# Joining seven expert accumulators later: stored raw, then added by GpSimd in the last network

## Chip, cores and metric

The kernel runs on one core of one Trainium2 chip. The metric is the device time of one execution in microseconds (us). TensorE does the matrix products, VectorE and ScalarE the elementwise work, GpSimd elementwise work on SBUF only, and SP's queue issues most transfers.

## The reference

The program chains three networks over 2304 tokens: an attention with random features, a mixture of eight experts, and a last two-layer network. Only the last two touch the change:

```python
# experts: x is (2304, 512), w1 (8, 512, 1024), w2 (8, 1024, 512)
out = np.zeros((N, D), dtype=np.float32)
for e in range(E):
    h = np.maximum(x @ w1[e], 0.0)
    ye = h @ w2[e]
    out += P[:, e:e + 1] * ye        # P: gate weights, after 8 rounds of normalisation
# last network: w_in (512, 2048), w_out (2048, 512)
h = x @ w_in
g = h - np.tanh(h)
return (g @ w_out).astype(np.float32)
```

All data are float32. The kernel splits each operand into a high part and a low part and takes three products (high x high, high x low, low x high) for each one above.

## The kernel before

Tokens are worked in three blocks of 768 (two halves of 384). The stages run in this order: attention; the experts for blocks 0, 1, 2; the last network for blocks 0, 1, 2.

**The experts in blocks 1 and 2.** The 8 x 1024 hidden units are cut into 32 quads of 256. A quad is multiplied by a scheme of seven products in place of eight (Strassen, in Winograd's form). `quad7` does the first layer: seven products into three PSUM banks, with gates and ReLU on VectorE, and seven operands `h7_*`, each split into high (ScalarE, L1286) and low (GpSimd, L1289). The second layer multiplies each of the seven operands by its own weights and sums over the quads into seven accumulators `seven0` to `seven6` in SBUF (`xacc`, 128 x 2 x 384 each, 384 KB). `group` is one such product for one half `d` of the rows. Where its flag `act` is set and the accumulator holds something, ScalarE first copies the accumulator into the PSUM bank (`pre`, L1372), the products add to it there, and ScalarE copies the bank back (L1396). Otherwise VectorE adds bank and accumulator (L1400). `second_layer` puts a quad's groups into a plan of numbered slots; `slot(t)` issues what is due at t, seven slots to a quad, and the second layer of a quad runs in the slots of the next.

**The end of a block.** The seven sums have to be combined into four results. In the last quad (`r == NQ - 1`) the groups get a list `outs`: each bank is preloaded with its own accumulator, and evicted by VectorE into another (L1394), for instance `xacc[3] <- bank` by ScalarE beside `xacc[5] <- bank + xacc[5]` by VectorE. `join` then has GpSimd make two more additions (L1416) and stores four results (L1413) into the DRAM tensor `xd[1]`, three on SP and one on ScalarE's queue. After block 1 this stands between the last quad of one block and the first of the next. After block 2 it stands in front of the last network: the eleven slots left over are spread over the first four `p` products of block 0 there, three, four and four at a time, through `second(...)`.

**The last network.** Groups of four hidden slices (`GF = 4`) and two token halves give half-groups. A half-group has four `shrink` calls (twelve `p` products each, L1481, an activation built from ScalarE and VectorE operations, L1493 to L1504, and a split of the hidden value into high on ScalarE, L1509, and low on GpSimd, L1510) and, some time later, three `l2` calls (twelve `l` products each, L1521, evicted by VectorE, L1546 or L1548). In `weights` the jobs `"i"` split the first layer's weights on GpSimd (`u`, L110), four units to a load, and the jobs `"s"` the second layer's (`v`), half on GpSimd and half on VectorE. `tick` advances these generators, `wprep` and `xprep`, one step.

**The next block's x.** `xops` (the generator `xprep`) loads the x of the coming block and splits it into units, by turns on VectorE and GpSimd (L110). For the last network it waits until `(1, s)` is in `xdone` and `xgo` allows it, that is, until the first group of the block before has been issued.

The lines that matter most:

```python
def pre():
    cell.append(lbank(f"Y{t}_{i}_{d}")[:, :TB])
    nc.scalar.copy(cell[0], xacc[i][:, d])
...
        one(4, 3, [(5, 5), (3, None)])
...
        at(t + 7)[2].extend((put(4, 0, 0), add(3, 2)))
        at(t + 8)[2].append(add(5, 1))
```

Of the kernel before, what the change touches and what calls it, by code (L numbers as in the profile page):

```python
# [20 lines left out]
def performer_moe_kernel(ctx, tc, q, k, v, omega, wg, w1, w2, win64, wout64, out):  # L21
# [6 lines left out]
    P = 128  # L28
# [47 lines left out]
    pt = con.tile([P, NTT, E], F32, name="pt")  # L76


    stages = [(0, s) for s in range(NSB)] + [(1, s) for s in range(NSB)]
# [95 lines left out]
    def second_units(R):  # L175
        r = R % NQ
        if r == 0:
            return [(0, R), (2, R), (1, R), (6, R), (3, R)]
        if r % 2 == 0:
            return [(0, R - 1), (0, R), (3, R), (2, R), (1, R), (6, R - 1), (6, R)]  # L180
        units = [(5, R - 1), (5, R), (4, R - 1), (4, R), (3, R), (2, R), (1, R)]
        return [(0, R), *units, (6, R)] if r == NQ - 1 else units

    def weights():
# [10 lines left out]
        for s in range(NSB):  # L195
            for g in range(NGM):
                for f in range(g * GF, (g + 1) * GF, 2):
                    jobs.append(("i", 0, lambda f=f: load_win(f), NCV if s else made["i", f]))
                for f in range(g * GF, (g + 1) * GF):
                    jobs.append(  # L200
                        (
                            "s",
                            -1,
                            lambda f=f: load_slab(wout32[f * P : (f + 1) * P, :]),
                            NCV if s else made["o", f],
                        )
                    )
# [38 lines left out]
        while ahead or jobs:  # L246
# [75 lines left out]
            elif k == "i":  # L322
                raw, done = raw
                for i in range(4):
                    while not free1(n1):
                        yield 1
                    o = i // 2 * P
                    unit1(n1, raw[:, i % 2 * 2 : i % 2 * 2 + 2, o : o + P], nc.gpsimd)
                    n1 += 1
                    yield None  # L330
# [31 lines left out]
    def xops():  # L362
        nx = 0
        order = []
        for k, (kind, s) in enumerate(stages):
            src = xd[kind].rearrange("(i c p) t -> p i c t", p=P, i=2)
            t0 = s * SBT
            opening = k == 0
            while not (opening or ready_x(kind, s) and k <= xgo[0]):
                yield 1  # L370
            b = {}

# [993 lines left out]

    def group(t, i, gs, d, act, first, last, outs=()):
        cell = []
# [5 lines left out]
        def run():  # L1374
# [13 lines left out]
            def evict():  # L1388
                if outs:
                    for x, y in outs:  # L1390
                        if y is None:
                            nc.scalar.copy(xacc[x][:, d], ps)
                        else:
                            nc.vector.tensor_tensor(xacc[x][:, d], ps, xacc[y][:, d], ALU.add)  # L1394
                elif act:
                    nc.scalar.copy(xacc[i][:, d], ps)  # L1396
# [6 lines left out]

        if (act or outs) and not first:
            at(t)[0].append(pre)
        at(t)[1].append(run)

    def join(s, t):
        to = xd[1].rearrange("(i c p) t -> p i c t", p=P, i=2)

        def put(x, r, c, eng=nc.sync):
            o = s * SBT + c * TB
            return lambda: eng.dma_start(to[:, r, :, o : o + TB], xacc[x])  # L1413

        def add(x, y):
            return lambda: nc.gpsimd.tensor_tensor(xacc[x], xacc[x], xacc[y], ALU.add)  # L1416

        at(t + 7)[2].extend((put(4, 0, 0), add(3, 2)))
        at(t + 8)[2].append(add(5, 1))
        at(t + 9)[2].append(put(6, 1, 0))  # L1420
        at(t + 10)[2].extend((put(3, 1, 1, nc.scalar), put(5, 0, 1), lambda: xdone.add((1, s))))

    def second_layer(s, R, post):
# [4 lines left out]

        def one(k, i, outs=()):
            first = r == 0  # L1430
            group(t + k, i, [R], 1, first or i in upper, first, False, outs)
            group(t + k, i, [R], 0, True, first, True, outs)

        def two(k, k2, i, outs=()):
            group(t + k, i, [R - 1, R], 1, True, r == 1, False, outs)
            group(t + k2, i, [R - 1, R], 0, True, r == 1, True, outs)

        if r == NQ - 1:
            one(1, 0)
            two(2, 3, 5, [(5, 0)])  # L1440
            two(3, 6, 4, [(4, 0)])
            one(4, 3, [(5, 5), (3, None)])
            one(5, 2, [(2, 0)])
            one(7, 1, [(2, 2), (1, None)])
            one(8, 6, [(6, 2)])
            join(s, t)
            return
        if r == 0:
            for k, i in ((1, 0), (4, 2), (5, 1), (6, 6), (7, 3)):
                one(k, i)  # L1450
# [190 lines left out]
    for st in stages:  # L1641
# [47 lines left out]
        elif kind == 0:  # L1689
# [40 lines left out]
            if s == NSB - 1:  # L1730
                while bg:
                    tick()
                ready.extend(lambda t=t: slot(t) for t in range(7 * NG, 7 * NG + 11))
                ready.append(last_turn)
        else:
            for g in range(NGM):
                for j in range(2):
                    hh = []
                    for f in range(GF):
                        for i in range(2):  # L1740
# [5 lines left out]
                                state["n1"] + 2 * f, j, f"{s}_{g}_{j}_{f}", early and f < 2,  # L1746
                                lambda: second((3, 4, 4, 0)[f] if early else 0),
                            )
# [63 lines left out]
```

## Time and profile before

| what | value |
|---|---|
| median of 3 runs | 2058.51 us (2058.39 to 2058.72) |
| the profiled execution | 2059.81 us, span 2058.0 us |
| TensorE busy | 2011.1 us, 98% of the span |
| VectorE, ScalarE, GpSimd busy | 1562.3, 1420.8, 1471.3 us |
| last network (about 1655 us to the end) | VectorE at 94.9% in a window from 1720 us |
| TensorE's mean granted clock | 0.998 |

The profile's rows are of one execution, with times in us from the start of its span unless they say ns. An engine that is busy need not be the one that sets the end: a row counts where TensorE waits, or where the work that it waits for stands.

### The profile page before, as it was taken

To read this page: it belongs to the slowest core of one execution; us is meant where nothing else is said; L and a number is where in the kernel's file an instruction comes from. 1 tells how busy PE (TensorE), PEld (TensorE's weight loads), DVE (VectorE), ACT (ScalarE), POOL (GpSimd) and SP (SyncE) were. 2 spreads that over 40 slices of the span, in tenths; PEclk is the share of its full clock that TensorE was granted. 3 is DMA by queue.
4 is the path that set the end of the run, shared out by engine and by line. 5 is a ranking of instruction groups with operands and counts; after the bars stand their busy time and mean duration, and the time that the engine had idled before them with its cause. 6 is when DMAs were issued, how large, how long until landed. Compare 5 with 4: busy or idle time off the path is not lost.

```text
span 2058.0 us, 37571 instructions
## 1 busy us (share of the span) xinstructions
PE 2011.1 (98%) x11408; PEld 1878.2 (91%) x11408; DVE 1562.3 (76%) x3004; ACT 1420.8 (69%) x3498; POOL 1471.3 (71%) x1855
## 2 busy tenths in 40 slices
PE   8999999999999999999999999999999989999999
PEld 7776888898999899999999999999999878989998
DVE  8885768889886665666666667777775589999997
ACT  7885333443442577777777688788788878888885
POOL 7885877887784588888888767676676675565652
PEclk9999999999999999999999999999999999999999
DMA  6545977798786688999988988988878532131310
GB/s 172 136 140 176 367 273 272 274 334 278 274 277 238 198 279 308 346 329 332 332 311 307 346 284 294 336 287 287 300 271 300 179 116 77 62 127 43 113 47 31
DMA packets 348056, 486.45 MB, mean 236 GB/s; under 512 B 71616, under 2 KB 166736, under 8 KB 347856
## 3 DMA queue, kind: packets, MB, share of 16 engines
q1 hardware_dynamic: 341712, 476.66, 67.6%
q10 hardware_dynamic: 6144, 7.40, 1.1%
q8 instruction: 92, 1.51, 0.3%
q14 instruction: 108, 0.88, 0.1%
HBM read 339.17 MB, written 144.78 MB: 235 GB/s over the span
## 4 chain that ended last, share of the span: by engine, by line
PE 79%; DVE 6%; POOL 6%; ACT 3%; issue 3%; DMA 2%; SPq 0%; ACTq 0%; DVEq 0%; POOLq 0%
PE l L1521 21%; PE Y L1380 18%; PE b L1205 13%; PE e L1205 9%; PE a L1205 8%; PE p L1481 7%; PE X L1380 2%; POOL tmp L616 2%; POOL eq L776 1%; POOL h L1289 1%; DMA y<-st 1%; DVE t L1502 0%; POOL u L110 0%; DVE t L1503 0%; DVE x L110 0%
## 5 line engine op out<-in xcount | busy, mean ns | idle before, releaser
L1380 PE MATMUL Y<-h,y 128*128 128x384 f32 x2394 | 486.3, 336 | 9.5 <-ACT Y L1372 9.0
L1521 PE MATMUL l<-v,h 128*128 128x512 f32 x2016 | 483.6, 393 | 8.9 <-POOL h L1510 3.8
L1521 PEld LDWEIGHTS l<-v,h 128*128 128x128 f32 x2016 | 375.5, 188 | 87.5 <-POOL h L1510 4.7
L1380 PEld LDWEIGHTS Y<-h,y 128*128 128x128 f32 x2394 | 419.9, 188 | 15.4 <-ACT Y L1372 14.5
L1289 POOL TENSOR_TENSOR h<-t,h 128x384 fp32r<-128x384 f32 x223 | 229.9, 1031 | 175.7 <-ACT h L1286 147.6
L1205 PE MATMUL b<-x,u 128*128 128x384 f32 x1728 | 348.5, 336 | 2.2 <-DVE t L1299 1.7
L1396 ACT COPY seven<-Y 128x384 f32<-128x384 f32 x534 | 247.1, 482 | 134.9 <-PE Y L1380 131.7
L1205 PEld LDWEIGHTS b<-x,u 128*128 128x128 f32 x1728 | 304.9, 188 | 8.0 <-DVE t L1299 2.0
L1372 ACT COPY Y<-seven 128x384 f32<-128x384 f32 x558 | 263.0, 488 | 3.8 <-DVE seven L1394 3.8
L1289 POOL TENSOR_TENSOR h<-h,h 128x384 fp32r<-128x384 f32 x192 | 203.6, 1066 | 43.3 <-ACT h L1286 40.1
L1205 PE MATMUL a<-x,u 128*128 128x384 f32 x1152 | 231.6, 335 | 1.6 <-POOL u L110 1.3
L1205 PE MATMUL e<-x,u 128*128 128x384 f32 x1152 | 231.2, 335 | 0.0
L1481 PE MATMUL p<-x,u 128*128 128x384 f32 x1152 | 210.6, 338 | 1.9 <-DVE seven L1394 1.9
L1481 PEld LDWEIGHTS p<-x,u 128*128 128x128 f32 x1152 | 203.8, 189 | 5.8 <-DVE seven L1394 2.2
L1205 PEld LDWEIGHTS a<-x,u 128*128 128x128 f32 x1152 | 202.3, 188 | 3.3 <-POOL u L110 1.7
L1205 PEld LDWEIGHTS e<-x,u 128*128 128x128 f32 x1152 | 202.5, 188 | 0.0
L110 POOL TENSOR_TENSOR v<-rs,v 128x256 fp32r<-128x256 f32 x176 | 144.0, 846 | 63.3 <-ACT v L107 54.9
L1510 POOL TENSOR_TENSOR h<-t,h 128x384 fp32r<-128x384 f32 x94 | 96.3, 1025 | 122.5 <-ACT h L1509 117.7
L1286 ACT CAST h<-t 128x384 fp32r<-128x384 f32 x224 | 115.7, 518 | 35.4 <-POOL t L1342 17.8
L1304 DVE TENSOR_TENSOR t<-b,t 128x384 f32<-128x384 f32 x64 | 35.6, 556 | 123.1 <-PE b L1205 123.1
L1556 DVE SCALAR_TENSOR_TENSOR acc<-l,pt,acc 128x512 f32<-128x512 f32 x144 | 104.7, 744 | 27.6 <-PE l L1521 25.9
L107 ACT CAST u<-s 128x256 fp32r<-128x256 f32 x128 | 49.4, 409 | 105.8 <-POOL u L110 42.0
(346 smaller groups left out, 3817.0 us busy)
## 6 DMA issues: line engine op xcount, KB each, us to landing
u<-st SPq DMA_DIRECT2D x448, 256.0 KB, 5.2
y<-st SPq DMA_DIRECT2D x336, 256.0 KB, 5.0
st<-u SPq DMA_DIRECT2D x224, 256.0 KB, 3.9
rs<-in_moe_w_dram SPq DMA_DIRECT2D x128, 256.0 KB, 4.8
st<-y SPq DMA_DIRECT2D x128, 256.0 KB, 5.7
st<-v SPq DMA_DIRECT2D x96, 256.0 KB, 5.2
rq<-in_moe_w_dram SPq DMA_DIRECT2D x32, 512.0 KB, 4.7
rqi<-win SPq DMA_DIRECT2D x24, 512.0 KB, 4.8
```

The costliest lines, as they stand in the source:

```text
L107: nc.scalar.copy(dst[:, 0], src)
L110: eng.tensor_tensor(dst[:, 1, i : i + w], src[:, i : i + w], dst[:, 0, i : i + w].bitcast(F32), ALU.subtract)
L1205: nc.tensor.matmul(ps[:, :TB], u[:, wi, c], x[:, xi, c], start=(start and m == 0), stop=(stop and m == 5), skip_group_check=True,)
L1286: nc.scalar.copy(H[k][:, 0], src)
L1289: eng.tensor_tensor(H[k][:, 1], src, H[k][:, 0].bitcast(F32), ALU.subtract)
L1372: nc.scalar.copy(cell[0], xacc[i][:, d])
L1380: nc.tensor.matmul(ps, uw[i, g][0][:, wi, d * P : (d + 1) * P], Hs[g][i][:, hi], start=(n == 0 and not cell), stop=(n == 3 * len(gs) - 1), ...
L1396: nc.scalar.copy(xacc[i][:, d], ps)
L1481: nc.tensor.matmul(ps, u1[f + i][:, wi, c], ux[state["x0"] + 2 * t + i][:, xi, c], start=(m == 0), stop=(m == 11))
L1510: nc.gpsimd.tensor_tensor(lo, s, hi.bitcast(F32), ALU.subtract)
L1521: nc.tensor.matmul(ps, hh[f][0][:, hi, t : t + P], u2[n + f][:, wi], start=(f == 0 and i == 0), stop=(f == len(hh) - 1 and i == 2),)
L1556: V.scalar_tensor_tensor(a, ps, p[:, e : e + 1], a, ALU.mult, ALU.add)
```

## The change

The last quad's `outs`, the preloads that belong to them and the two additions right behind it go. In the last quad of the last block (`fast`) the groups of accumulators 0, 3, 2, 1 and 6 are evicted by plain VectorE additions with no preload; those of 5 and 4, and all of block 1's last quad, stay as in any other quad. `keep_sums` stores the seven accumulators as they are into DRAM tensors `sv`, on SP, one by one from slot 2 to slot 9. A new `join` within `xops` loads them again in the last network, when the first group of the block before has been issued; GpSimd makes seven additions of 128 x 768 elements, one for every two ticks, and SP stores the four results to `xd[1]`, from which x is then loaded as before.

Three smaller things go with it: the order of the groups (and of the weight units that feed them) in a block's first quad; ten slots left over in place of eleven, spread three, three and four; and every other weight unit of the last network's very first group is split by VectorE in place of GpSimd.

```diff
+    sv = {(s, i): dp.tile([P, 2, TB], F32, name=f"sv{s}_{i}") for s in range(1, NSB) for i in range(7)}
...
-            return [(0, R), (2, R), (1, R), (6, R), (3, R)]
+            return [(0, R), (3, R), (2, R), (1, R), (6, R)]
...
-                    jobs.append(("i", 0, lambda f=f: load_win(f), NCV if s else made["i", f]))
+                    jobs.append(("i", not (s or g), lambda f=f: load_win(f), NCV if s else made["i", f]))
...
-                    unit1(n1, raw[:, i % 2 * 2 : i % 2 * 2 + 2, o : o + P], nc.gpsimd)
+                    unit1(n1, raw[:, i % 2 * 2 : i % 2 * 2 + 2, o : o + P], nc.vector if a and i % 2 else nc.gpsimd)
...
+        def join(s):
...
+            def get(i):
+                m[i] = xtp.tile([P, 2, TB], F32, tag="x", name=f"m{s}_{i}")
+                nc.sync.dma_start(m[i], sv[s, i])
+
+            def put(i, r, c):
+                o = s * SBT + c * TB
+                nc.sync.dma_start(to[:, r, :, o : o + TB], m[i])
+
+            for i in (0, 4, 1, 2, 6):
+                get(i)
+            for _ in range(6):
+                yield None
+            steps = [(4, 0), ("put", 4, 0, 0), (1, 0), ("get", 3), (2, 1), ("get", 5), (6, 2), ("put", 6, 1, 0)]
+            steps += [(5, 3), (3, 2), ("put", 3, 1, 1), (5, 1), ("put", 5, 0, 1)]
+            for x in steps:
...
+                    G.tensor_tensor(m[x[0]], m[x[0]], m[x[1]], ALU.add)
+                    yield None
+                    yield None
...
-            while not (opening or ready_x(kind, s) and k <= xgo[0]):
+            what = ("sums", s) if kind and s else (kind, s)
+            while not (opening or what in xdone and k <= xgo[0]):
                 yield 1
+            if what[0] == "sums":
+                yield from join(s)
...
-        if (act or outs) and not first:
+        if act and not first:
             at(t)[0].append(pre)
...
+    def keep_sums(s, t):
+
+        def put(i):
+            return lambda: nc.sync.dma_start(sv[s, i], xacc[i])
+
+        for k, i in ((2, 0), (4, 5), (5, 3), (6, 2), (7, 4), (8, 1), (9, 6)):
+            at(t + k)[2].append(put(i))
+        at(t + 9)[2].append(lambda: xdone.add(("sums", s)))
...
+            first, fast = r == 0, g_last == R
+            group(t + k, i, [R], 1, first or i in upper and not fast, first, False)
+            group(t + k, i, [R], 0, not fast, first, True)
...
-            two(2, 3, 5, [(5, 0)])
-            two(3, 6, 4, [(4, 0)])
-            one(4, 3, [(5, 5), (3, None)])
-            one(5, 2, [(2, 0)])
-            one(7, 1, [(2, 2), (1, None)])
-            one(8, 6, [(6, 2)])
-            join(s, t)
+            two(2, 3, 5)
+            two(3, 6, 4)
+            one(4, 3)
+            one(5, 2)
+            one(7, 1)
+            one(8, 6)
+            keep_sums(s, t)
...
-                ready.extend(lambda t=t: slot(t) for t in range(7 * NG, 7 * NG + 11))
+                ready.extend(lambda t=t: slot(t) for t in range(7 * NG, 7 * NG + 10))
...
-                                lambda: second((3, 4, 4, 0)[f] if early else 0),
+                                lambda: second((3, 3, 4, 0)[f] if early else 0),
```

## Rows read from the trace of the kernel before

**Rows 1.** The page, busy time, share and instructions of each engine.

```profile
PE 2011.1 (98%) x11408; PEld 1878.2 (91%) x11408; DVE 1562.3 (76%) x3004; ACT 1420.8 (69%) x3498; POOL 1471.3 (71%) x1855
```

**Rows 2.** Windows: stretch, length, busy us (and instructions) by engine, clock, DMA share, GB/s.

```profile
1170.00:1180.00 10.00, 7.88 (x46) 7.56 (x45) 4.90 (x10) 4.29 (x10) 9.38 (x9) 1.00 0.87 304
1625.80:1673.95 48.15, 37.46 (x186) 33.99 (x187) 34.00 (x53) 38.09 (x90) 36.66 (x39) 0.93 0.44 147
1652.00:1669.00 17.00, 11.75 (x59) 10.21 (x59) 13.65 (x21) 12.59 (x29) 16.57 (x16) 0.94 0.26 92
1670.00:1680.00 10.00, 10.00 (x41) 8.94 (x41) 7.92 (x12) 8.77 (x21) 6.85 (x7) 0.81 0.84 301
1720.00:1820.00 100.00, 99.85 (x505) 90.70 (x505) 94.92 (x150) 83.85 (x186) 60.34 (x64) 1.00 0.29 95
```

**Rows 3.** TensorE's timeline at boundary A: start, us, what, [idle before <- releaser].

```profile
1177.04 1.14 PE L1380 MATMUL X<-h,y 128*128 128x384 f32 x5 [2.12 <-POOL h L1289]
...
1185.88 1.31 PE L1380 MATMUL X<-h,y 128*128 128x384 f32 x6 [0.39 <-ACT seven L1396]
```

**Rows 4.** TensorE's groups, 1625.80 to 1673.95: count, busy, mean ns, idle before, releaser.

```profile
L1481 PE MATMUL p<-x,u 128*128 128x384 f32 x108 | 21.5, 356 | 1.9 <-DVE seven L1394 1.9
L1380 PE MATMUL Y<-h,y 128*128 128x384 f32 x63 | 12.9, 345 | 4.4 <-ACT Y L1372 4.4
L1521 PE MATMUL l<-v,h 128*128 128x512 f32 x12 | 4.0, 445 | 4.3 <-POOL h L1510 3.8 <-ACT h L1509 0.5
```

**Rows 5.** The chain of waits in the last network: start, us, what.

```profile
1725.91 5.48 PE l L1521 x24
1731.39 6.26 PE p L1481 x36
...
1742.53 5.48 PE l L1521 x24
```

**Rows 6.** TensorE's timeline at boundary B and just after it.

```profile
1653.55 8.66 PE L1481 MATMUL p<-x,u 128*128 128x384 f32 x48 [1.92 <-DVE seven L1394]
...
1670.23 3.89 PE L1481 MATMUL p<-x,u 128*128 128x384 f32 x12
...
1703.85 2.99 PE L1521 MATMUL l<-v,h 128*128 128x512 f32 x12 [1.42 <-ACT h L1509]
```

**Rows 7.** TensorE's timeline around the second x split.

```profile
1820.57 2.92 PE L1521 MATMUL l<-v,h 128*128 128x512 f32 x12
...
1837.86 3.00 PE L1521 MATMUL l<-v,h 128*128 128x512 f32 x12 [0.51 <-ACT h L1509]
```

**Rows 8.** Windows from one lone `l` eviction of VectorE to the next.

```profile
1684.54:1703.02 18.48, 17.89 (x92) 16.10 (x90) 17.65 (x27) 14.18 (x28) 9.72 (x9) 1.00 0.00 1
1752.35:1767.65 15.30, 15.30 (x79) 13.82 (x78) 14.47 (x24) 12.69 (x29) 8.17 (x9) 1.00 0.01 2
1767.65:1784.64 16.99, 16.99 (x88) 15.51 (x87) 16.16 (x27) 14.41 (x32) 11.06 (x12) 1.00 0.39 124
1816.94:1837.04 20.10, 20.10 (x106) 18.60 (x105) 19.27 (x27) 15.71 (x33) 13.89 (x13) 1.00 0.15 52
```

**Rows 9.** VectorE's timeline around the second x split.

```profile
1812.56 0.69 DVE L110 TENSOR_TENSOR v<-rs,v 128x512 fp32r<-128x512 f32 x1
...
1816.94 0.68 DVE L1546 COPY acc<-l 128x512 f32<-128x512 f32 x1
...
1837.04 0.67 DVE L1546 COPY acc<-l 128x512 f32<-128x512 f32 x1
```

**Rows 10.** What writes or reads `seven`: count, ns min/median/max, first and last start.

```profile
L1372 ACT COPY Y<-seven x558: 468/487/531, 718.0 to 1646.4; 128x384 f32<-128x384 f32 x186
...
L1394 DVE TENSOR_TENSOR seven<-Y,seven x24: 539/543/558, 1157.0 to 1653.4; 128x384 f32<-128x384 f32 x24
...
L1416 POOL TENSOR_TENSOR seven<-seven,seven x4: 1843/1847/1857, 1169.2 to 1655.6; 128x768 f32<-128x768 f32 x4
```

**Rows 11.** GpSimd's groups, 1625 to 1669: count, busy, mean ns, idle before, releaser.

```profile
L110 POOL TENSOR_TENSOR u<-rqi,u 128x256 fp32r<-128x256 f32 x16 | 13.5, 863 | 1.6 <-ACT u L107 0.9 <-DMA rs<-wout 0.7
```

More of the change, by code (lines that the diff above doesn't have):

```diff
@@ L364, in xops @@
         order = []
+        def join(s):
+            G = nc.gpsimd
+            to = xd[1].rearrange("(i c p) t -> p i c t", p=P, i=2)
+            m = {}
+            def get(i):
[11 more added lines that the diff above has]
+            for x in steps:
+                if x[0] == "put":
+                    put(*x[1:])
+                elif x[0] == "get":
+                    get(x[1])
+                else:
+                    G.tensor_tensor(m[x[0]], m[x[0]], m[x[1]], ALU.add)
+                    yield None
+                    yield None
+            xdone.add((1, s))
         for k, (kind, s) in enumerate(stages):
@@ L1365, in slot, with group @@
         plan.pop(t)
-    def group(t, i, gs, d, act, first, last, outs=()):
+    def group(t, i, gs, d, act, first, last):
         cell = []
@@ L1388, in evict @@
             def evict():
[L1389 to L1395, printed above, removed]
+                if act:
                     nc.scalar.copy(xacc[i][:, d], ps)
@@ L1402, in run @@
             return evict
-        if (act or outs) and not first:
+        if act and not first:
             at(t)[0].append(pre)
         at(t)[1].append(run)
[L1408 to L1421, printed above, removed]
+    def keep_sums(s, t):
[4 more added lines that the diff above has]
+        at(t + 9)[2].append(lambda: xdone.add(("sums", s)))
     def second_layer(s, R, post):
@@ L1427, in second_layer, with one, two @@
         upper = (1, 2, 3) if s == 2 else (2,)
[L1429 to L1436, printed above, removed]
+        def one(k, i):
+            first, fast = r == 0, g_last == R
+            group(t + k, i, [R], 1, first or i in upper and not fast, first, False)
+            group(t + k, i, [R], 0, not fast, first, True)
+        def two(k, k2, i):
+            group(t + k, i, [R - 1, R], 1, True, r == 1, False)
+            group(t + k2, i, [R - 1, R], 0, True, r == 1, True)
+        g_last = NG - 1
         if r == NQ - 1:
             one(1, 0)
-            two(2, 3, 5, [(5, 0)])
-            two(3, 6, 4, [(4, 0)])
-            one(4, 3, [(5, 5), (3, None)])
-            one(5, 2, [(2, 0)])
-            one(7, 1, [(2, 2), (1, None)])
-            one(8, 6, [(6, 2)])
-            join(s, t)
+            two(2, 3, 5)
[5 more added lines that the diff above has]
+            keep_sums(s, t)
             return
         if r == 0:
-            for k, i in ((1, 0), (4, 2), (5, 1), (6, 6), (7, 3)):
+            for k, i in ((1, 0), (4, 3), (5, 2), (6, 1), (7, 6)):
                 one(k, i)
```

## The prediction

> **What bounds the kernel now.** I read the page first: TensorE is busy 98% of the span [rows 1], so a change can only give back stretches in which TensorE waits or runs slowly, or make new ones. The list of what TensorE waited for and the windows then show where these are. In the middle of the last network nothing is lost: in the window from 1720 us TensorE is busy 99.85 of 100 us, but VectorE is busy 94.9 of the same 100 [rows 2]. The reader is to see that there is almost no room on VectorE there. The losses that this change touches are three.
>
> *Boundary A, blocks 1 to 2 of the experts (about 1170 to 1190 us).* TensorE waits 2.12 us for a GpSimd `h` split and 0.39 us for a ScalarE copy [rows 3], while GpSimd is busy 9.38 of 10 us [rows 2].
>
> *Boundary B, the experts' last block to the last network (1625.80 to 1673.95 us).* The window is 48.15 us long and holds 63 + 108 recorded matmuls of 384 columns, 3 more that start a bank anew, and 12 of 512 columns [rows 4]. At the undisturbed pace, 6.26 us for 36 and 5.48 us for 24 [rows 5], these are 174 x 0.174 + 12 x 0.228 = 33.0 us. So about 15 us are lost: 4.4 us in waits for the ScalarE copy that preloads a PSUM bank, 1.9 for VectorE's last evictions, 4.3 for the `h` splits of the layer just begun [rows 4], and the rest in matmuls that are spread out or at a lower clock: the granted clock is 0.81 from 1670 to 1680 us after those waits [rows 2], between the levels of 1.2 and 2.4 GHz, and twelve matmuls took 3.89 us there [rows 6].
>
> *Two short stalls in the last network*, 1.42 us [rows 6] and 0.51 us [rows 7], each in the half-group in which `xops` splits the next block's x. VectorE is the cause. A half-group takes TensorE 16.6 us (from one pair of `l` products to the next, 1725.91 to 1742.53) [rows 5]. VectorE needs 15.30 and 16.99 us by turns, but 20.10 and 18.48 us with an x split in it [rows 8]. Before that split it evicted its lone `l` bank at 1817.6 us, 3.0 us before TensorE asked for it; in the next round it was late [rows 7, 9].
>
> **The change part by part.** The sum is made against the profiled execution, 2059.81 us, which is 1.3 us above the median of the runs shown (2058.51).
>
> *Boundary A.* The combining evictions, the two 1.85 us additions [rows 10] and the four stores of results go. Seven stores of the sums come, 384 KB each as the old four were, so 1.2 MB more where the transfer share is already 0.87 at 304 GB/s [rows 2]: 3.8 us of transfer. I cost that at nothing because two quads of weights are in the rings ahead of it; with that cover gone it costs up to 3.8 us. SP waits at each store for its eviction, and the weight loads queue behind; the same rings hide it. The last quad becomes an ordinary one, like the thirty before it. Each sum is stored at least five slots (10 us) before the next block overwrites it. I take the whole 2.5 us back (bounds 0 and 2.5).
>
> *Boundary B.* In the old code, thirteen groups of the last quad are preloaded by ScalarE at 0.488 us, and twelve evictions are VectorE's combining additions [rows 10]. Now only four are preloaded, ten evictions are plain VectorE additions and four are copies. ScalarE loses nine preloads and one eviction, 10 x 0.48 = 4.8 us; VectorE goes from thirteen evictions to ten. GpSimd loses 3.7 us of additions and its wait for the data. Four of its 16 weight splits there, 13.5 us in all [rows 11], go to VectorE: 3.4 us less on GpSimd, about 1.5 us more (estimate: half a 0.69 us split of 512 columns [rows 9] each) on a VectorE that is busy only 34.0 of 48.15 us [rows 2], so hidden. SP no longer holds its queue until GpSimd's last addition; it waits for evictions instead, with the loads of the next weights behind them, which were issued late for the same reason. I add up three steps. The `p` products that begin at 1653.55 us [rows 6] can begin when the last evictions are done; 27.75 us pass before them for 102 matmuls of 0.174 us, 17.7 us, so 10 are lost. Of these I take back 5.4: the preload waits and part of the eviction wait; what remains is that VectorE runs the activation of one `p` ahead of those evictions. Next, GpSimd, busy 16.57 of 17 us up to 1669 us [rows 2], is 3.7 us earlier at the `h` splits that `l` waits for: 3.0 us of the waits go. Last, with shorter gaps the clock holds: 3.89 us become about 2.3, 1.6 us. Together 10.0 us. The bounds are 5 us (GpSimd's 3.7 us and most of the clock alone) and 15 us (all of the loss).
>
> *The additions in the last network.* Each of blocks 1 and 2 now has seven loads, seven GpSimd additions and four stores, from the first group of the block before on, one addition for each `p` product. The transfers are hidden: the share is 0.29 there [rows 2]. The stores wait on SP for GpSimd with weight loads behind them; weights are split a whole group of two half-groups (33 us) ahead, so I cost this at nothing; without that cover each wait would cost up to an addition, 1.85 us. TensorE waits for nothing of it directly, since the sums are needed 60 us or more later.
>
> What the additions can cost is VectorE time: its three operations on SBUF operands get longer while GpSimd runs. No row shows a 1.85 us addition among them. The nearest are the two x splits. They held four GpSimd pieces of 384 columns, the columns of two additions. The excess over 15.30 us is 4.8 and 3.2 us [rows 8]; VectorE's own two pieces of 768 columns are an estimated 2 x 1.03 us (1.5 times the 0.69 us of 512 columns [rows 9]). That leaves 2.7 and 1.1 us, or 1.35 and 0.55 us for each addition. I take the middle, 0.95 us: 6.7 us for seven. Below nothing is excluded, since GpSimd only gets work there; the highest value is the whole addition, 1.85 us: 13 us.
>
> From that VectorE can absorb its lead and what it regains, 33.2 - 32.3 = 0.9 us in two half-groups, about 1.8 us over the join and the x split. The x split itself still costs 4.0 us (mean of 4.8 and 3.2). In the first of the two blocks I give VectorE a lead of 3.0 us (it leaves boundary B earlier by more than TensorE does), in the second 1.6 us, regained since. Stalls: 6.7 + 4.0 - 3.0 - 1.8 = 5.9 us, and 6.7 + 4.0 - 1.6 - 1.8 = 7.3 us; 13.2 us, in place of 1.9 us now (1.42 and 0.51). So +11.3 us.
>
> This is where a rule of the Trainium skill bears. SBUF — State Buffer, section "SBUF: two separate sides", says that GpSimd and VectorE operations with two SBUF inputs take a shared pair of ports by an exclusive lock, and the one that comes second waits for the whole instruction. The longer VectorE operations agree with it in kind; by it alone each addition could cost VectorE 1.85 us, not 0.95, and the sum would be 12.6 us higher.
>
> The order of the groups in a block's first quad and of the weight units that feed it change together, and cost nothing.
>
> Sum: -2.5 - 10.0 + 11.3 = -1.2 us, 2058.6 us for the profiled execution, 2057.3 us against the median.
>
> **The rivals.**
>
> *1. Each addition blocks VectorE for nearly all of its length* (slower). For it: VectorE has 0.9 us to spare in 33, and the x split in block 1 cost 1.35 us per addition's worth. Against it: the other one cost 0.55, and adds may fall on VectorE's PSUM operations. At 1.85 us: 13 us a join, stalls of 12.2 and 13.6, less 1.9, so -12.5 + 23.9 = +11.4 us, 2069.9 us. It decides from 1.33 us for each addition on, where the sum passes +4.1 us. The rule of the Trainium skill above (SBUF — State Buffer, "SBUF: two separate sides") would bring this about.
>
> *2. The additions are mostly hidden* (faster). GpSimd is busy 60 of 100 us [rows 2], and its weight splits in the 15.30 us half-groups cost VectorE little. At 0.55 us: 3.9 us a join, stalls 3.1 and 4.5, less 1.9: -12.5 + 5.7 = -6.8 us, 2051.7 us. It decides below 0.74 us. Against it: weight splits of 0.86 us [rows 11] leave gaps between them that a 1.85 us addition doesn't.
>
> *3. The change doesn't do what it says at boundary B*: VectorE's activation chain stands before the last evictions in either order, TensorE gets only 5 us of the 15 back, and the sum is +3.8 us, 2062.3 us.
>
> **How the numbers follow.** Forecast of a near balance 0.35, rival 2 0.32, rival 1 0.25, rival 3 0.08. A measurement of this kernel can tell about 0.2%, 4.1 us, from no change: below 2054.4 faster, above 2062.6 slower. Forecast and rival 3 lie within: same 0.43, faster 0.32, slower 0.25. The forecast's own range is 2054.4 to 2062 us. With the unknown costs at their ends (all of boundary B and 0.55 us an addition, -12 us; 5 us and 1.85 us, +16 us) the extremes are 2046.7 and 2074.9; leaving a tenth out on either side, the range is 2049 to 2067 us.
>
> **What would show it.** Right: no wait for `Y L1372` and no clock under 1.00 at boundary B, the first `p` run of the second half-group starting 5 us earlier after the last expert product; no GpSimd wait near 1177 us. In the last network, stalls of `l` products behind VectorE's evictions in the two blocks with joins, some 13 us in all, with longer L1502 to L1504 operations beside the additions. Wrong: half-groups with additions still near 15.3 and 17 us (rival 2), or over 20 us (rival 1); SP held so long by a store that weight splits come late, with TensorE waiting for `u` or `v` in place of `l` evictions; a boundary B in which the `p` run still waits for an eviction (rival 3).

## The result, and the profile after

The kernel became slower: 2080.8 us (median; 2078.84 to 2083.06) beside 2058.61 us of the kernel before on the same chip, a ratio of 1.0106 (95% interval 1.0089 to 1.0124). The prediction was 2057.3 us with a range of 2049 to 2067. The profiled execution took 2078.84 us with a span of 2076.7 us.

I cut both spans at the same matrix products: A from the 63rd to the 74th group of `e` products in blocks 1 and 2 of the experts, B from the last `e` group to the first pair of `l` products (24 of them), J1 and J2 the next eight half-groups each, from pair to pair. J1 and J2 hold one join each. Lengths in us:

| kernel | up to A | A | between | B | J1 | J2 | to the last `l` | tail | span |
|---|---|---|---|---|---|---|---|---|---|
| before | 1139.4 | 85.1 | 400.1 | 49.4 | 134.9 | 134.0 | 94.8 | 20.4 | 2058.0 |
| after | 1138.3 | 89.0 | 400.1 | 40.2 | 147.6 | 146.6 | 94.8 | 20.1 | 2076.7 |
| after less before | -1.1 | +3.9 | 0 | -9.2 | +12.7 | +12.6 | 0 | -0.3 | +18.7 |

The stretch up to A differs by up to 4.7 us among executions of kernels that don't differ there, so its -1.1 says nothing. A isn't steady either where SP issues the stores of the sums: it took 86.1 to 89.7 us in this execution and in those of `late`, `late_noadd` and `late_vec` below, which don't differ there, beside 85.1 to 86.0 us in the five executions that combine block 1 as before. So the loss at A is some 1 to 4 us. The table already tells the rest: boundary B gave nearly what was forecast (-10.0), boundary A lost where 2.5 us were to be gained, and the two joins cost 25.3 us in place of 11.3.

The page after, busy time and share of each engine, beside [rows 1]:

```profile
PE 2018.3 (97%) x11408; PEld 1882.8 (91%) x11408; DVE 1572.3 (76%) x2996; ACT 1416.8 (68%) x3490; POOL 1495.5 (72%) x1861
```

The shares hardly move, so they explain nothing; the windows do. The view is that of [rows 2], with the same columns:

```profile
1170.00:1180.00 10.00, 10.00 (x59) 10.00 (x59) 5.84 (x10) 5.21 (x12) 8.03 (x8) 1.00 0.86 320
1150.00:1200.00 50.00, 45.99 (x249) 45.67 (x248) 24.01 (x45) 29.04 (x69) 26.27 (x26) 0.93 0.90 332
1660.00:1680.00 20.00, 20.00 (x104) 18.26 (x103) 19.07 (x27) 17.38 (x40) 17.32 (x17) 1.00 0.57 203
1700.00:1720.00 20.00, 15.88 (x80) 13.99 (x78) 19.14 (x23) 11.78 (x26) 19.32 (x15) 1.00 0.47 155
1720.00:1740.00 20.00, 18.07 (x68) 15.17 (x69) 14.59 (x21) 14.90 (x32) 12.65 (x13) 0.74 0.26 89
```

**Boundary A.** From 1170 to 1180 us TensorE no longer waits: the old stall is gone. A new one stands a few us later, in the window that reaches to 1200. TensorE's timeline there, beside [rows 3]:

```profile
1180.58 1.21 PE L1241 MATMUL b<-x,u 128*128 128x384 f32 x6
1185.79 2.29 PE L1416 MATMUL X<-h,y 128*128 128x384 f32 x6 [4.01 <-ACT seven L1426]
1187.87 2.12 PE L1241 MATMUL e<-x,u 128*128 128x384 f32 x6
```

It waits 4.01 us for a ScalarE eviction, and the next groups of six take 2.29 and 2.12 us, not the 1.21 us of the group before. ScalarE's timeline names what ScalarE waited for:

```profile
1185.26 0.86 ACT L1426 COPY seven<-X 128x384 f32<-128x384 f32 x2 [6.57 <-DMA sv<-seven]
...
1188.80 1.24 ACT L1426 COPY seven<-X 128x384 f32<-128x384 f32 x3 [1.89 <-DMA sv<-seven]
```

The next block may not overwrite accumulators 1 and 6 until their stores have read them. ScalarE's last eviction of the old sums ended at 1169.87 us; SP's queue issued the last two stores (L1441) only here, among weight loads (L292, L314):

```profile
1175.47 0.33 SPq L1441 DMA_DIRECT2D sv<-seven  x1
1176.06 0.77 SPq L314 DMA_DIRECT2D y<-st  x1
1176.88 1.56 SPq L292 DMA_DIRECT2D u<-st  x1
1178.49 0.94 SPq L314 DMA_DIRECT2D y<-st  x1
1182.00 0.32 SPq L292 DMA_DIRECT2D u<-st  x1
1183.02 0.32 SPq L1441 DMA_DIRECT2D sv<-seven  x1
```

1175.47 us and the end of the first wait are 9.8 us apart, 1183.02 and the end of the second 5.8; block 1's seven stores took 5.1, 5.9 and 9.7 us (minimum, median, maximum) to land.

**Boundary B.** TensorE's timeline, beside [rows 6]:

```profile
1629.51 1.34 PE L1416 MATMUL Y<-h,y 128*128 128x384 f32 x6 [0.96 <-ACT Y L1408]
...
1636.30 1.31 PE L1416 MATMUL Y<-h,y 128*128 128x384 f32 x6 [1.29 <-ACT Y L1408]
...
1654.22 8.61 PE L1506 MATMUL p<-x,u 128*128 128x384 f32 x48 [1.21 <-DVE seven L1430]
1662.67 2.92 PE L1546 MATMUL l<-v,h 128*128 128x512 f32 x12
1665.43 2.27 PE L1506 MATMUL p<-x,u 128*128 128x384 f32 x12
1667.54 4.74 PE L1546 MATMUL l<-v,h 128*128 128x512 f32 x20
```

The last `e` product is 2.7 us later than before (1627.34 for 1624.58), yet the first pair of `l` begins 6.4 us earlier. Two waits for a preload of ScalarE (L1408, the old L1372) and one for the last eviction are still there. But the 48 `p` products run straight into the `l` products, with no wait for GpSimd's `h`; twelve `p` take 2.27 us in place of 3.89, and the clock of the window is 1.00 where [rows 2] had 0.81.

**The joins.** First the additions, by tile (count, ns minimum/median/maximum), then VectorE's timeline beside them:

```profile
L393 POOL TENSOR_TENSOR m<-m,m x14: 1844/2160/2290, 1688.5 to 1859.8; 128x768 f32<-128x768 f32 x14
```

```profile
1685.61 0.56 DVE L1528 SCALAR_TENSOR_TENSOR t<-t,t 128x384 f32<-128x384 f32 x1
1686.27 0.60 DVE L1529 COPY_PREDICATED t<-t,th 128x384 f32<-128x384 uint32 x1
...
1689.06 2.02 DVE L1528 SCALAR_TENSOR_TENSOR t<-t,t 128x384 f32<-128x384 f32 x1
...
1693.93 2.02 DVE L1528 SCALAR_TENSOR_TENSOR t<-t,t 128x384 f32<-128x384 f32 x1
1696.05 2.00 DVE L1529 COPY_PREDICATED t<-t,th 128x384 f32<-128x384 uint32 x1
...
1700.28 2.02 DVE L1528 SCALAR_TENSOR_TENSOR t<-t,t 128x384 f32<-128x384 f32 x1
...
1704.91 0.54 DVE L1521 TENSOR_TENSOR th<-p,th 128x384 f32<-128x384 f32 x1
```

GpSimd made four additions from 1688.49 to 1701.88 us, and four VectorE operations that read only SBUF took 2.00 or 2.02 us in place of 0.56 or 0.60: 1.40 to 1.46 us for each of these additions. The fifth, from 1703.88 to 1705.73 us, fell mostly on operations that read PSUM, and they kept their 0.54 us (L1521). VectorE has no such room [rows 2], and TensorE stalls behind its evictions:

```profile
1709.56 6.43 PE L1506 MATMUL p<-x,u 128*128 128x384 f32 x36
1720.11 3.42 PE L1546 MATMUL l<-v,h 128*128 128x512 f32 x9 [4.13 <-DVE acc L1573]
1725.35 1.88 PE L1546 MATMUL l<-v,h 128*128 128x512 f32 x3 [1.82 <-ACT h L1534]
1727.02 4.04 PE L1506 MATMUL p<-x,u 128*128 128x384 f32 x12
```

The window from 1720 has a clock of 0.74. Part of the stall has another cause, which ScalarE's timeline shows:

```profile
1722.29 0.83 ACT L109 CAST x<-xt 128x768 fp32r<-128x768 f32 x1 [3.90 <-DMA xt<-xd]
1723.03 0.48 ACT L1518 ACTIVATE t<-p 128x384 f32<-128x384 f32 x1
```

The reload of the next block's x had only been issued from 1717.69 us on, since it stands behind the last additions and their stores, and the x split waited for it at the head of ScalarE's queue, with the activations of `p` products behind it. The second join has the same wait, 4.30 us.

### The profile page after: what moved, and what is told of

Its sections match the earlier page's. It is cut to its first block, busy times and chain, and to the rows that moved or that the text cites. A ratio compares the mean times of both kernels' runs of the same rounds, so it can differ in the third digit from the quotient of the medians.

```text
span 2076.7 us, 37593 instructions
## 1 busy us (share of the span) xinstructions
PE 2018.3 (97%) x11408; PEld 1882.8 (91%) x11408; DVE 1572.3 (76%) x2996; ACT 1416.8 (68%) x3490; POOL 1495.5 (72%) x1861
## 4 chain that ended last, share of the span: by engine, by line
PE 73%; POOL 8%; DVE 7%; issue 4%; ACT 4%; DMA 3%; SPq 0%; ACTq 0%; DVEq 0%; POOLq 0%
PE Y L1416 18%; PE l L1546 17%; PE b L1241 13%; PE e L1241 9%; PE a L1241 9%; PE p L1506 4%; PE X L1416 2%; POOL tmp L652 2%; POOL u L112 1%; POOL eq L812 1%; POOL h L1535 1%; DMA y<-st 1%; DVE t L1520 1%; POOL v L112 1%; DVE t L1528 1%
## 5 line engine op out<-in xcount | busy, mean ns | idle before, releaser
L1416 PE MATMUL Y<-h,y 128*128 128x384 f32 x2358 | 479.2, 335 | 7.3 <-ACT Y L1408 6.8
L1546 PEld LDWEIGHTS l<-v,h 128*128 128x128 f32 x2016 | 377.2, 189 | 104.3 <-ACT h L1534 12.6
L1416 PEld LDWEIGHTS Y<-h,y 128*128 128x128 f32 x2358 | 413.9, 188 | 12.1 <-ACT Y L1408 11.1
L1426 ACT COPY seven<-Y 128x384 f32<-128x384 f32 x546 | 252.7, 481 | 139.4 <-PE Y L1416 135.6
L1408 ACT COPY Y<-seven 128x384 f32<-128x384 f32 x546 | 257.5, 488 | 0.0
L109 ACT CAST u<-s 128x256 fp32r<-128x256 f32 x128 | 49.4, 409 | 105.9 <-POOL u L112 42.0
```

What stands on the lines that cost most here:

```text
L109: nc.scalar.copy(dst[:, 0], src)
L1416: nc.tensor.matmul(ps, uw[i, g][0][:, wi, d * P : (d + 1) * P], Hs[g][i][:, hi], start=(n == 0 and not cell), stop=(n == 3 * len(gs) - 1), ...
L1546: nc.tensor.matmul(ps, hh[f][0][:, hi, t : t + P], u2[n + f][:, wi], start=(f == 0 and i == 0), stop=(f == len(hh) - 1 and i == 2),)
```

## The experiments

Theory 1 after this reading: an addition on GpSimd takes 1.4 us from VectorE, the late reload stops ScalarE once a join, and the late stores stop it at boundary A. The rivals: the reload alone makes the joins long; the joins are long by their transfers and waits, whoever adds; the stores are late by the traffic, not by SP's order. Ratios are to the kernel before on the same chip, in brackets their 95% intervals.

| run | median us | ratio | A | B | J1 | J2 |
|---|---|---|---|---|---|---|
| `late` | 2069.54 | 1.0043 (1.0028 to 1.0058) | 89.7 | 40.2 | 143.3 | 141.9 |
| `late_noadd` | 2050.11 | 0.9956 (0.994 to 0.9971) | 86.1 | 40.1 | 134.3 | 133.2 |
| `late_vec` | 2061.55 | 1.0007 (0.9997 to 1.0017) | 88.2 | 40.1 | 139.9 | 138.5 |
| `old_a` | 2065.04 | 1.0022 (1.0013 to 1.0032) | 85.5 | 41.4 | 136.2 | 145.4 |
| `best` | 2056.49 | 0.9977 (0.9967 to 0.9987) | 86.0 | 40.2 | 135.7 | 137.3 |
| `best_spread` | 2059.2 | 0.999 (0.998 to 1.0) | 86.0 | 41.4 | 143.5 | 133.3 |
| `best_spread_g` | 2062.08 | 1.001 (1.0 to 1.0019) | 85.7 | 41.3 | 146.7 | 133.3 |
| `vec_actq` | 2054.6 | 0.9966 (0.9952 to 0.998) | 81.9 | 40.2 | 139.8 | 138.7 |
| `dma_add` | 2063.14 | 1.0007 (0.9997 to 1.0017) | 81.9 | 40.2 | 144.1 | 142.2 |
| `dma_add_wide` | 2053.88 | 0.9962 (0.9949 to 0.9975) | 81.8 | 40.2 | 141.2 | 134.5 |
| `dma_wide_x5` | 2053.66 | 0.9968 (0.9955 to 0.998) | 81.8 | 40.1 | 141.3 | 134.1 |
| `dma_wide_x20` | 2049.13 | 0.9948 (0.9933 to 0.9962) | 81.9 | 40.2 | 136.6 | 135.8 |

**`late`: the x split eight steps further behind its load.**

```diff
-                for _ in range(1 if s else 4):
+                for _ in range(9 if what[0] == "sums" else 1 if s else 4):
```

> The changed kernel, with the four x splits behind each join issued eight generator steps (four p products, about 16 us) later, so that the reloaded x has landed. In the changed kernel each join costs 12.7 us. Theory 1 (the additions block VectorE, and the wait for the reload comes on top): ScalarE's waits of 3.9 and 4.3 us for the x load go, and the waits of the l products behind them; each join falls to about 8 us, some 2071 us. Theory 2 (the joins cost so much because ScalarE stands still behind the late load, the additions themselves are mostly hidden): each falls to about 2 us, some 2059 us.

ScalarE's waits for x are gone and the joins fall by 4.3 and 4.7 us: that is the price of the late reload. The edit also moves the split itself, which can count too (`dma_wide_x20`, below); no run parts the two. Some 8 us a join over before remain, so the reload alone is not the cause.

**`late_noadd`: the same without the additions.** It leaves out all fourteen, so that blocks 1 and 2 of the last network work on raw sums; loads, stores and reloads stay.

```diff
-                    G.tensor_tensor(m[x[0]], m[x[0]], m[x[1]], ALU.add)
```

> As late, with the seven additions of each join left out (loads and stores stay; the output of blocks 1 and 2 is then made of raw sums). Theory 1: VectorE's operations are no longer held, so each join falls by 6 to 8 us against late, to 1 or 2 us; some 2056 to 2058 us. Theory 2: within 3 us of late.

The joins fall below those of before, to 134.3 and 133.2 us: the seven additions cost 9.0 and 8.7 us a join, more than the 6 to 8 us expected, and the twenty-two transfers of the two joins nothing that shows. The windows J1 and J2 (columns as in [rows 2]), first in `late`, then without the additions, show where it goes:

```profile
1667.95:1811.22 143.27, 135.49 (x673) 121.76 (x673) 136.53 (x196) 112.17 (x246) 99.67 (x92) 0.99 0.33 112
1811.22:1953.09 141.87, 136.40 (x674) 122.96 (x674) 135.24 (x195) 111.97 (x247) 98.50 (x93) 0.98 0.34 114
```

```profile
1664.92:1799.27 134.35, 133.50 (x673) 120.85 (x673) 127.61 (x196) 111.74 (x246) 83.61 (x85) 1.00 0.36 121
1799.27:1932.44 133.17, 133.13 (x673) 120.98 (x673) 126.27 (x195) 111.80 (x246) 82.94 (x86) 1.00 0.36 121
```

With the same number of instructions VectorE is busy 8.9 and 9.0 us longer, 1.27 and 1.28 us for an addition as the average of all seven, and the joins grow by as much. VectorE's L1528 (here L1527) from 1680 to 1704 us, first in `late`, then without the additions (count, busy us, mean ns, idle before):

```profile
L1528 DVE SCALAR_TENSOR_TENSOR t<-t,t 128x384 f32<-128x384 f32 x5 | 7.7, 1542 | 0.5
```

```profile
L1527 DVE SCALAR_TENSOR_TENSOR t<-t,t 128x384 f32<-128x384 f32 x6 | 3.4, 558 | 0.6
```

**`late_vec`: `late` with the additions on VectorE.**

```diff
-            G = nc.gpsimd
+            G = nc.vector
```

> As late, with the additions made by VectorE itself in place of GpSimd. Theory 1: an addition holds VectorE for 1.4 us when GpSimd makes it and takes VectorE about 0.96 us itself (the duration of an undisturbed piece of 768 columns), so the joins get cheaper by 7 x 0.45 = 3 us each: some 6 us below late. Theory 2 (GpSimd's additions hidden): VectorE, which has no room, takes 7 us more for each join: some 10 us above late.

8 us faster than `late`, some 3.4 us of it in each join (the rest mostly at A, where the two don't differ). One addition takes VectorE 0.95 us:

```profile
L393 DVE TENSOR_TENSOR m<-m,m x14: 940/946/1484, 1688.8 to 1849.0; 128x768 f32<-128x768 f32 x14
```

So the engine that was to be spared loses more when GpSimd adds (1.27 us each) than when it adds itself. Its busy time in the windows J1 and J2 is 132.76 and 131.72 us here, 3.8 and 3.5 us less than in `late`, and the joins are shorter by nearly that.

**`old_a`: block 1 combined as before, block 2 by the new way.** The old `outs`, preloads, `join` and order of groups come back for every block but the last:

```diff
+        if r == NQ - 1 and s < NSB - 1:
+            one(1, 0)
+            two(2, 3, 5, [(5, 0)])
...
+            join_here(s, t)
+            return
```

> Block 1's sums are combined as in the kernel before (preloads, combining evictions, two GpSimd additions, order of the first quad's groups), block 2's as in the changed kernel. If the three places add up independently, the store wait at the boundary of blocks 1 and 2 (3.9 us) and the first join (12.7 us) go: 2080.8 - 16.6 = 2064 us, and the second boundary keeps its gain of 9 us and the second join its 12.7. Rival: the second join's cost depends on the VectorE backlog that the first leaves, and falls to 8 us or less with it: below 2060 us.

J1 loses its 11 us and A its 3.5; B and J2 keep theirs to within 1.2 us. The places add up.

**`best`: `old_a`, `late` and `late_vec` together.** No line is new.

> Block 1 combined as in the kernel before (as in old_a), block 2 stored and joined in the last network with VectorE's additions and the later x split (as in late_vec). From the runs so far: the second boundary gives 9 us back, and a join made so costs about 4 us in late_vec ((2061.6 - 2058.6 + 1.1 - 3.9 + 9.2) / 2 = 4.7). Theory 1 and independent places: 2058.6 - 9.2 + 4.7 = 2054 us. Rival: the gain at the second boundary only pays for a VectorE backlog that comes back later, and the time is that of the kernel before, 2058 to 2060 us.

It is faster than before by 0.23%: boundary B's 9 us less one join on VectorE, 3.3 us, and 1.7 us by which A and J1 came out longer. That is 4.4 us under before, where 4.6 were expected.

**`best_spread` and `best_spread_g`: block 2's join begun a stage earlier, one addition to six steps; the second with the additions back on GpSimd.**

```diff
-                    yield None
-                    yield None
+                    for _ in range(6):
+                        yield None
...
-            while not (opening or what in xdone and k <= xgo[0]):
+            while not (opening or what in xdone and k - (what[0] == "sums") <= xgo[0]):
...
-            G = nc.vector
+            G = nc.gpsimd
```

> As best, with block 2's join begun a whole stage earlier (as soon as block 1's x is split) and one addition every six generator steps in place of two. If what a join costs is only what VectorE cannot absorb at once, seven additions of 0.96 us over some 21 p products find the 0.45 us that VectorE regains in each half-group and its lead: the join falls from 4.7 to 1 or 2 us, 2051 to 2052 us. Rival (each addition costs its time wherever it stands): as best within 1 us.

> As best_spread, with the additions on GpSimd. Theory 1 (an addition holds VectorE for 1.4 us): 7 x 0.45 = 3 us more VectorE time, of which the spread absorbs part: 0 to 3 us above best_spread. Theory 2 (spread out, GpSimd's additions are hidden): 2 us or more below best_spread, since VectorE does nothing for them.

The first missed: it is 2.7 us slower than `best`, where some 3 us were to be gained. J2 gives back 4.0 us, but J1 takes 7.8 more. The edit moved more than the additions, though: block 2's x is split right behind its join, so that split came along, from 1856.56 us on in `best` to 1780.05 us on here. J1 now holds seven additions and two x splits, J2 none of either, and what of the 7.8 us is the additions' no run shows. The second agrees with `late_vec`: on GpSimd the same additions cost 3 us more.

**`vec_actq`: `late_vec` with two of block 1's stores, those of accumulators 1 and 6, issued by ScalarE.**

```diff
-            return lambda: nc.sync.dma_start(sv[s, i], xacc[i])
+            eng = nc.scalar if s < NSB - 1 and i in (1, 6) else nc.sync
+            return lambda: eng.dma_start(sv[s, i], xacc[i])
```

> As late_vec, with block 1's last two stores (accumulators 1 and 6) issued by ScalarE's queue in place of SP's. In the changed kernel TensorE lost 4.0 us at the first boundary because ScalarE waited 6.6 and 1.9 us for these stores before it could overwrite the accumulators; the first of them was issued 5.6 us after its data was there, behind weight loads on SP. If the late issue is the cause: these waits shrink by 4 us or more, and the time falls 3 to 4 us below late_vec, to 2058 us. If the landing in a full DMA system is (9.7 us from issue): the wait stays, within 1 us of late_vec.

A falls from 88.2 to 81.9 us, 3.2 under that of before. ScalarE's queue issues the stores right behind the evictions, and in the window that had 45.99 busy us TensorE is now never idle:

```profile
1168.69 0.33 ACTq L1442 DMA_DIRECT2D sv<-seven  x1
1169.85 0.33 ACTq L1442 DMA_DIRECT2D sv<-seven  x1
```

```profile
1150.00:1200.00 50.00, 50.00 (x291) 50.00 (x290) 28.57 (x54) 35.99 (x86) 30.46 (x31) 1.00 1.00 371
```

The traffic is no less (371 GB/s here, 332 there) and block 1's stores take as long to land (5.3, 6.0 and 9.5 us), so it was the order on SP that made the stores late. The Trainium skill, DMA: Bandwidth & Descriptors, section "Issuing engines are not separate DMA queues", says that another issuing engine saves only the time that its sequencer takes to start a transfer, usually little. Two issues of 0.33 us agree with the last words; but 6.3 us came back here, because what a store stands behind in SP's order counts too.

**`dma_add`: `vec_actq` with the additions made by accumulating transfers in place of VectorE's instructions.**

```diff
-            G = nc.vector
+            G = nc.gpsimd
...
-                    G.tensor_tensor(m[x[0]], m[x[0]], m[x[1]], ALU.add)
+                    G.dma_start(m[x[0]], m[x[1]], accum_op=ALU.add)
```

> vec_actq with the seven additions of each join made by accumulating transfers issued by GpSimd (tile to tile in SBUF), in place of VectorE's additions; no engine adds anything in the joins. Theory 1 (a join costs what its additions take from VectorE, and nothing else of it costs anything once x is reloaded late): the two joins fall from 139.8 and 138.7 us to near the 134.3 and 133.2 us of late_noadd, so the time is 5.5 + 5.5 us under vec_actq, 2043 to 2046 us. Theory 2 (the work only moves: GpSimd has to issue fourteen more transfers, and as it works in order it waits at those that need the sum before, so the weight splits and the hidden values' low parts behind it come late): the joins stay at 139 us or more, 2054 us or more, with TensorE waiting for POOL h in the joins and VectorE's operations at their usual 0.56 to 0.60 us.

Theory 2 of this run holds. Each transfer that needs an earlier sum waits at the head of GpSimd's queue; the tile's view for the first join, VectorE's timeline and TensorE's:

```profile
its engine sat idle before it (us, times) until:
  DMA m<-m: 11.2, 3
```

```profile
1702.02 0.56 DVE L1521 TENSOR_TENSOR t<-t,p 128x384 f32<-128x384 f32 x1 [6.27 <-POOL h L1536]
```

```profile
1714.42 5.46 PE L1547 MATMUL l<-v,h 128*128 128x512 f32 x12 [7.81 <-ACT t L1524]
```

**`dma_add_wide`: the seven transfers in four batches, six steps apart.**

```diff
+            steps = [(4, 0), (1, 0), 6, ("put", 4, 0, 0), ("get", 3), ("get", 5), (2, 1), 6]
+            steps += [(6, 2), (5, 3), 6, ("put", 6, 1, 0), (3, 2), (5, 1), 6, ("put", 3, 1, 1), ("put", 5, 0, 1)]
...
+                if x == 6:
+                    for _ in range(6):
+                        yield None
...
-                    yield None
-                    yield None
```

> dma_add with its seven accumulating transfers of a join issued in four batches, six steps of the generator (some 9 to 10 us; the transfers landed within 8.9 us) between a batch and the next, so that no transfer waits on GpSimd for the one whose sum it needs. Theory 1 (dma_add lost its gain to GpSimd standing still for 11.2 us in the first join and 10.4 us in the second, with the hidden values' splits behind): GpSimd waits no longer for the tile m, the joins fall from 144.1 and 142.2 us to near the 134.3 and 133.2 us of late_noadd, and the time is 2043 to 2046 us. Theory 2 (accumulating transfers cost something else, for instance the 14 issues of 0.87 us on GpSimd hold VectorE as its additions did, or their traffic delays the weights): the joins stay at 139 us or more, 2054 us or more, with VectorE operations of SBUF operands longer than 0.60 us beside the issues.

GpSimd waits for no `m` any more, and J2 is 134.5 us, beside 133.2 without additions. But the time missed the 2043 to 2046 us expected, since J1 keeps one stall, in the half-group of the x split; TensorE's timeline, and the window of the products behind it:

```profile
1746.21 5.46 PE L1548 MATMUL l<-v,h 128*128 128x512 f32 x12 [4.20 <-DVE acc L1575]
```

```profile
1746.21:1751.67 5.46, 5.46 (x13) 4.31 (x14) 5.25 (x9) 4.16 (x11) 5.46 (x7) 0.50 0.01 2
```

A wait of 4.20 us costs 6.7: the twelve products behind it ran at a granted clock of 0.50 (1.2 GHz) and took 5.46 us, not the 2.92 to 3.00 of [rows 7].

**`dma_wide_x20` and `dma_wide_x5`: the x split moved later and earlier.**

```diff
-                for _ in range(9 if what[0] == "sums" else 1 if s else 4):
+                for _ in range(20 if what[0] == "sums" else 1 if s else 4):
```

(4 in place of 20 in the other.)

> dma_add_wide with the reloaded x split twenty steps after its load is issued in place of nine, some 17 us later (1752 us in the first join), where GpSimd has no weights to split in the profile of dma_add_wide. Theory 1 (what is left in dma_add_wide's joins, 141.2 and 134.5 us, is the x split falling among ten u splits of GpSimd, which stretch VectorE's two x pieces to 1.75 us and L1529 to 1.4 us): the first join falls to 134 to 136 us, VectorE's x pieces take some 0.95 to 1.35 us, and the time is 2047 to 2050 us. Theory 2 (the x split costs VectorE the same wherever it falls, and the stall comes from the lead that VectorE has then): the first join stays at 139 us or more, 2052 to 2056 us.

> dma_add_wide with the reloaded x split four steps after its load is issued in place of nine, some 8 us earlier (about 1727 us in the first join), among the v splits of GpSimd and VectorE and before the u splits. Theory 1 (the stall hangs on how many weight splits of GpSimd stand beside the x split): between dma_add_wide and dma_wide_x20, first join 136 to 140 us, 2049 to 2053 us. Theory 2 (it hangs on VectorE's lead alone): as dma_add_wide, 141 us, 2052 to 2056 us. A wait of ScalarE for the tile xt would show that the load was not there yet (landing 3.5 to 4.2 us).

Later, the first join is 136.6 us, the second 135.8, and the time 2049.13 us, the fastest of all, 0.52% under before. VectorE's two x pieces by tile, in `dma_add_wide` and then in `dma_wide_x20`, and the stall that is left in the latter:

```profile
L112 DVE TENSOR_TENSOR x<-xt,x x2: 1745/1758/1770, 1737.8 to 1743.7; 128x768 fp32r<-128x768 f32 x2
```

```profile
L112 DVE TENSOR_TENSOR x<-xt,x x2: 939/1346/1752, 1750.8 to 1755.2; 128x768 fp32r<-128x768 f32 x2
```

```profile
1756.93 3.00 PE L1548 MATMUL l<-v,h 128*128 128x512 f32 x12 [1.01 <-DVE acc L1575]
```

Behind a wait of 1.01 us the products kept their pace. But `dma_wide_x5` doesn't bear out the explanation by weight splits: with pieces of 1.27 and 1.77 us its first join is 141.3 us, as in `dma_add_wide`, with a wait of 4.14 us, there for ScalarE's `h`. That the later place is worth 4.6 us in J1 and takes 1.3 us back in J2 is shown; what makes a place good is left open.

## Why the prediction was wrong

Three steps failed: the cover of the stores at boundary A, the price of one addition, and the reload of x, which no term held.

**Boundary B: the total was right, its parts were not.** Forecast -10.0, measured -9.2. The first step, up to the run of 48 `p` products, was to give 5.4 us. It gave 2.1, 25.68 us (1628.54 to 1654.22) in place of 27.75: two preload waits and the wait of 1.21 us for the last eviction remain, and the second is a sign that I had named for rival 3. There was also less to gain: I counted 102 matmuls in that stretch, but with 66 of the experts and four `p` products there are 114, 19.8 us, so 7.9 us were lost and not 10. The two later steps, the `h` waits and the clock, were to give 4.6 us and gave 7.1: from there to the first pair of `l` it is 13.32 us in place of 20.40, which leaves almost no loss. So their mechanism held, and that the sum came within 0.8 us was in part luck. Rival 3 (5 us only) falls.

**Boundary A: wrong sign, -2.5 forecast, +3.9 measured (+1.0 to +4.6 over the four executions).** The 2.12 us wait for GpSimd did go. The step that failed is the cover: "Each sum is stored at least five slots (10 us) before the next block overwrites it". I priced the traffic of the stores and the loads queued behind them, and counted the slots from the store's place in the plan. But SP works its list in order and issued the last two stores 5.6 and 13.2 us after the last eviction had ended, and then a store took up to 9.8 us. The overwriting copy, which waits for the store, is ScalarE's, and TensorE's banks stand behind ScalarE. `vec_actq` shows the cause: with the stores issued in time the 2.5 us, and a little more, are there (81.9 us beside 85.1).

**The additions: the price of one was mis-sized.** I took 0.95 us of VectorE's time, the middle of 0.55 and 1.35; the average of all seven is 1.27 to 1.28 (`late` less `late_noadd`), near the upper bound and just under the 1.33 from which rival 1 decides. The 1.40 to 1.46 us hold where an addition falls on an operation that reads only SBUF. My own formula with 1.28 gives 7 x 1.28 = 9.0 us a join, stalls of 8.2 and 9.6 us, less 1.9: +15.8 us for +11.3. Measured is 9.0 + 8.7 us from `late_noadd` to `late`, less the 1.4 us by which the joins of `late_noadd` are shorter than those of before: 16.3. So the structure (VectorE's lead eats a part, the rest becomes stalls of TensorE) held and the term didn't. By this term alone the sum would have been +3.3 us, 2061.8 us, within the range; A and the reload took it out. Why the middle of the two x splits was too low is argued, not shown: their GpSimd pieces are 384 columns long, and a shorter piece may hold VectorE for less.

Of this the Trainium skill spoke (SBUF — State Buffer, section "SBUF: two separate sides"): an operation of GpSimd and one of VectorE with two SBUF inputs exclude each other for the whole instruction. The trace agrees: 0.56 became 2.02 us, and an operation with a PSUM input stayed at 0.54. An addition that falls on such an operation costs little, so the average is 1.28 us and not the 1.85 that I worked out from the rule. I gave that rule a quarter of the chance, and the nearer rows, which could not show it, more.

**What I missed in the joins: the reload.** "The transfers are hidden: the share is 0.29" is right of bandwidth, and `late_noadd` shows it. But the chain of additions and stores pushes the x load behind it, and a split then waits 3.90 and 4.30 us for it on ScalarE: 4.3 and 4.7 us of the joins, 9.0 in all, by `late` (with what moving the split brings in it). It wasn't in the sum, nor in a rival.

The account against the sum: A 6.4 us worse, B 0.8, the joins 14.0 (5.0 for the price, 9.0 for the reload), together 21.2, less 1.4 us by which the stretch up to A and the tail came out shorter: 19.8 of the 19.9 us between -1.2 and +18.7. Rival 1's direction and cause were right, but its 1.85 us an addition were not reached, nor quite its 1.33, and its 2069.9 us lacked A and the reload. Rival 2, which needs less than 0.74, is excluded.

The idea of storing raw sums was sound. Its 9 us at boundary B and 3 at boundary A are real, and with additions made by transfers, two stores on another queue and a later x split the kernel is at 2049.13 us (0.9948 of before).

## What to carry to other kernels

Work taken off VectorE and given to GpSimd isn't off VectorE: find the VectorE operations with SBUF operands beside it, and price a long GpSimd instruction by most of its length there: here 1.28 us of 1.85 on average, and up to 1.46 us. When a buffer is stored and then reused, count from the issue that its queue can really make to the landing, not from the slot in a plan, and look for who stands behind the engine that must wait. An operand that is loaded late stops everything behind the first instruction that needs it, so move the use, not only the load.

## What the runs showed of the hardware

An addition of 768 columns held a VectorE operation that reads only SBUF for 1.40 to 1.46 us when GpSimd made it; over seven additions it was 1.27 to 1.28 us each. VectorE makes the same addition in 0.95 us. Accumulating transfers of 384 KB from SBUF to SBUF, issued by GpSimd in 0.86 to 1.18 us each, landed after 5.3 us (median, `dma_add_wide`) and once none was waited for, a join with them took 134.5 to 141.2 us, beside 133.2 and 134.3 without additions. Behind waits of about 4 us twelve `l` products took 5.46 us at a clock of 0.50, which adds more than half to the price of the wait; behind one of 1.01 us they took 3.00.
